# Own and early values in one 64-row product: a memory-augmented recurrent attention kernel

## Chip, cores and metric

The kernel runs on one core of a Trainium2 chip. The metric is the device time of one execution in microseconds; the median of several runs is given.

## The reference

`h = x + A(layernorm(x))`, `out = h + B(layernorm(h))`, with x of 2048 tokens by 640, bf16.

B is a gated feed-forward: `(relu(n @ W_gate) * (n @ W_up)) @ W_down`, with 1728 hidden columns.

A is attention over segments of 32 tokens, one after the other, 32 heads of 128. Each segment sees 8 memory rows, and its first 8 output rows are the memory of the next:

```python
mem = mem0
for s in range(n_seg):                      # 64 segments of 32
    h = concatenate([mem, x[:, 32*s:32*s+32]], axis=1)      # 8 + 32 rows
    q, k, v = h @ Wq, h @ Wk, h @ Wv                        # 32 heads of 128
    scores = where(idx_q < 8 or idx_q >= idx_k, q @ k.T * scale, -1e9)
    o = (softmax(scores) @ v) @ Wo
    mem = o[:, :8]
    outs.append(o[:, 8:])
```

So memory rows see all 40 keys, and a token sees the memory and the tokens up to itself. The chain from `mem` to the next `mem` is serial over 64 segments.

## The kernel before

The weights Wq, Wk, Wv and Wo stay in SBUF. A segment's 40 keys are split in two sets. The *own* keys are the 8 memory rows and the first 24 tokens, 32 rows that need the new memory. The *early* keys are the last 8 tokens (RID = 24) of four consecutive segments, 32 rows that need no memory; their K, Q and V (`Ke`, `Qe`, `Ve`) are computed once for four segments, in units (`extra_units`, `filler`) that lie between the steps of the segments before. In every fourth segment the gaps are filled with `woe_pass`, the output product of early rows.

All these products use tiles of 128 rows by 32 columns: four column groups run side by side, and the four groups g of eight heads each come out in the partitions 32g to 32g + 31. A head is written (k, g), k from 0 to 7.

A segment s of the main loop (line 898) goes, in the order of the code:

- K product (`project`, L374) in two halves, each copied from PSUM by ScalarE (`to_tok`, L395, into `tok[0]`, `tok[1]`) and transposed by VectorE into `Ko` (`flip`, L390).
- `pv_x(s - 1, 0)` (L629 to L643): values for the 32 token rows of the segment before. For each head one product with the own values (`Vp`) and one with the early values (`Ve`), 32 rows each, on tiles of 32x32; the second is added to the first in PSUM. Row group g writes bank b0 + g. 64 matmuls.
- `norm_x` (L645): reciprocal and two multiplications on VectorE into `ox`; `flip_ox` (L532) later transposes `ox` into `oT`.
- Q product, its copies into `tok[2]`, `tok[3]` and flips; half of the V product, copied to `Vp` by ScalarE (`to_v`).
- `scores` (L450) half 0, the second half of V, `scores` half 1: 32 products of 128x32 by 40 columns a half, own keys (a = 0) at column offset 0 and early keys (a = 1) at 160.
- `exp_mem`, `mask_mem`, `pv_mem` (L505), `norm_mem`, `flip_mem`: the 8 memory queries, both halves; between them `exp_x`, `mask_x` for the 32 token queries, and fillers on TensorE.
- `wo_split` (L560), `fold_split`, `wo_pass` (L547), `to_act_split` (L593): the output product, which gives the next segment's memory rows in `act_r`; `rows_split` and `store_attn` send the token rows to DRAM.

The program order is written out by hand. `_Graph` derives the semaphores: each operation waits for the writers and readers of its keys on other engines and for DMAs; every engine runs its own operations in order. SP issues nearly all DMAs, in the order of the code. `store_attn` issues four per segment, and every fourth segment adds a DMA transpose of the next normalised rows and a load.

The first segment is handled in a prologue (L859 to L896) while the last weights are loaded. After segment 63 the feed-forward follows, whose weights are loaded in pieces (`load_piece`) during segments 62 and 63.

Of the kernel before, what the change touches and what calls it, by code (L numbers as in the profile page):

```python
# [163 lines left out]
def build_kernel(nc, A_x, A_mem0, A_Wq, A_Wk, A_Wv, A_Wo, A_seg_len, B_W_gate, B_W_up, B_W_down, out):  # L164
# [57 lines left out]
    mca = ar.alloc("mca", [128, 5, SEG], BF16)  # L222
    act_r = [ar.alloc(f"act_r{i}", [128, 4, DC, 32], BF16) for i in range(2)]
    act_e = [ar.alloc(f"act_e{i}", [128, DC, 32], BF16) for i in range(2)]
    tok = [ar.alloc(f"tok{i}", [128, 512], BF16) for i in range(4)]
# [5 lines left out]
    Vp = [ar.alloc(f"Vp{i}", [128, 8, VW], BF16) for i in range(2)]  # L231
# [8 lines left out]
    ox = ar.alloc("ox", [128, 4, 2, Dh], BF16)  # L240
    wtok = [ar.alloc(f"wtok{i}", [128, DC, 32], BF16) for i in range(2)]
# [36 lines left out]
    for i in (1, 0):  # L278
        add("pool", lambda p, i=i: p.memset(wtok[i][:], 0.0), w=[("wtok", i)])
# [4 lines left out]
    for i in range(2):  # L284
        add("dve", lambda v, i=i: v.memset(oT[i][:], 0.0), w=[("oT", i, n, kh) for n in "mx" for kh in range(2)])
        add("pool", lambda p, i=i: p.memset(act_r[i][:], 0.0),
            w=[("act", i, j, "m") for j in range(4)] + [("act", i, "x")] + [("act", i, "x", j) for j in range(4)])
        add("pool", lambda p, i=i: p.memset(ap(Vp[i], Dh, [[VW, 8], [1, VW - Dh]]), 1.0), w=[("Vp1", i)])
        add("pool", lambda p, i=i: p.memset(ap(Ve[i], Dh, [[VW, 8], [1, VW - Dh]]), 1.0), w=[("Ve1", i)])
        add("pool", lambda p, i=i: p.memset(act_e[i][:], 0.0), w=[("acte", i)])  # L290

    add("pool", lambda p: p.memset(mca[:], BIG), w=[("mca",)])
    for g in range(4):
        for n in range(5):
            sl = mca[32 * g:32 * g + 32, n, :]
            add("pool", lambda p, sl=sl, n=n: p.affine_select(sl, sl, [[1, SEG]], ALU.is_ge, 0.0,
                                                              base=M if n == 0 else M * (n - 1) - RID,
                                                              channel_multiplier=-1), r=[("mca",)], w=[("mca",)])
            if n > 1:
                add("pool", lambda p, sl=sl, n=n: p.affine_select(sl, sl, [[0, SEG]], ALU.is_ge, 0.0,  # L300
                                                                  base=-M * (n - 1), channel_multiplier=1),
                    r=[("mca",)], w=[("mca",)])
    add("pool", lambda p: p.memset(mbd[:], 0.0), w=[("mbd",)])
    for g in range(4):
        add("pool", lambda p, g=g: p.memset(mbd[32 * g:32 * g + 32, :, 8 * g:8 * g + 8], BIG), r=[("mbd",)], w=[("mbd",)])
        for n in range(1, 5):
            sl = mbd[32 * g:32 * g + 32, n, :]
            add("pool", lambda p, sl=sl, n=n: p.affine_select(sl, sl, [[0, 32]], ALU.is_ge, 0.0, base=-M * (n - 1),
                                                              channel_multiplier=1), r=[("mbd",)], w=[("mbd",)])
            add("pool", lambda p, sl=sl, n=n: p.affine_select(sl, sl, [[0, 32]], ALU.is_ge, 0.0, base=M * n - 1,  # L310
                                                              channel_multiplier=-1), r=[("mbd",)], w=[("mbd",)])
# [51 lines left out]
    def project(act, akeys, j, halves, banks, chunks=range(5)):  # L363

        def f(pe):
            for c in chunks:
                for n, i in enumerate(halves):
                    for g in range(4):
                        o = 2048 * i
                        w = (W[:, j, c, o + 512 * g:o + 512 * g + 512] if j == 2 else  # L370
                             W[:, j, c, o:o + 2048].rearrange("p (h e) -> p h e", e=128)[:, :, 32 * g:32 * g + 32])
                        a = (bank(banks[n])[32 * g:32 * g + 32, :], act[:, c, :], w)
                        if n == 0 or not HOLD:
                            ins = pe.matmul(*a, start=(c == 0), stop=(c == DC - 1), skip_group_check=True)  # L374
                        else:
                            ins = again(pe, *a, c == 0, c == DC - 1, g)
            return ins
        add("pe", f, r=list(akeys) + [("W", j, c) for c in chunks], w=[B(b) for b in banks] + [("Wdone", j)])
# [71 lines left out]
    def scores(s, hf):  # L450

        p, _ = place(s)

        def f(pe):
            for k in range(4 * hf, 4 * hf + 4):
                for a in range(2):
                    for g in range(4):
                        h = head(k, g)
                        o = 160 * a + 40 * (k % 4)
                        i = pe.matmul(bank((P0, P1)[hf])[32 * g:32 * g + 32, o:o + 40],  # L460
                                      (Ko if a == 0 else Ke[p])[:, h, :], Qo[:, h, :], start=True, stop=True,
                                      skip_group_check=True)
            return i
        add("pe", f, r=[("Ko", hf), ("Qo", hf), ("Qo", "e"), ("Ke", p, hf)], w=[B((P0, P1)[hf])])
# [9 lines left out]
    def exp_mem(s, hf):  # L474
        _, j = place(s)
        add("act", lambda a: a.activation(ap(Pm, 32 * hf, [[64, 2], [8, 4], [1, 8]]), s_view(hf, 0, M), ACTF.Exp,
                                          scale=SCALE), r=[B((P0, P1)[hf])], w=[("Pm", hf)])

    def mask_mem(s, hf):
        _, j = place(s)  # L480
        for i in (1, 0):
            add("dve", lambda v, i=i: v.tensor_tensor(ap(Pbd, 256 * i + 128 * hf, [[32, 4], [8, 4], [1, 8]]),
                                                      ap(Pm, 64 * i + 32 * hf, [[8, 4], [0, 4], [1, 8]]),
                                                      ap(mbd, 32 * (1 + j) * i, [[0, 4], [8, 4], [1, 8]]), ALU.min),
# [7 lines left out]
    def mask_x(s):  # L492
# [3 lines left out]
                                             ap(mca, 0, [[32 * (1 + j), 2], [0, 8], [1, 32]]), ALU.min),  # L496
            r=[("Px", 0), ("Px", 1), ("mca",)], w=[("Px", 0), ("Px", 1)])

    def v_of(s, a):
        par, p = s % 2, place(s)[0]  # L500
        if a == 0:
            return Vp[par], [("Vp", par, i) for i in range(2)] + [("Vp1", par)]
        return Ve[p], [("Ve", p, i) for i in range(2)] + [("Ve1", p)]

    def pv_mem(s, hf):  # L505
# [10 lines left out]
        (vp, e), par = place(s), s % 2  # L516
        add("pe", f, r=[("Pbd", a, hf) for a in range(2)] + [("Ve", vp, hf), ("Ve1", vp), ("Vp", par, hf), ("Vp1", par)],
# [14 lines left out]
    def flip_ox(s, halves=(0, 1)):  # L532
        p = (s + 1) % 2
        for kh in halves:
            add("dve", lambda v, kh=kh: v.transpose(ap(oT[p], 160 * kh + M, [[320, 4], [40, 4], [1, 32]]),  # L535
                                                       ap(ox, 128 * kh, [[256, 4], [1, 4], [4, 32]])),
                r=[("ox", kh)], w=[("oT", p, "x", kh)])
# [90 lines left out]

    def pv_x(s, b0):  # L629
        (t0, k0), (t1, k1) = v_of(s, 0), v_of(s, 1)  # L630

        def f(pe):
            for kh in range(2):
                for a in range(2):
                    for c in range(4):
                        k = 4 * kh + c
                        for g in range(4):
                            i = pe.matmul(bank(b0 + g)[32 * c:32 * c + 32, 129 * kh:129 * kh + 129],  # L638
                                          Px[32 * g:32 * g + 32, 256 * a + 32 * k:256 * a + 32 * k + 32],
                                          (t0, t1)[a][32 * g:32 * g + 32, k, 0:129], start=(a == 0), stop=(a == 1),  # L640
                                          skip_group_check=True, tile_position=(32 * g, 32 * c))
            return i
        add("pe", f, r=[("Px", 0), ("Px", 1)] + k0 + k1, w=[B(b0 + g) for g in range(4)])  # L643

    def norm_x(b0):  # L645
        src = ps[:, b0 * 512:b0 * 512 + 2048].rearrange("p (g r) -> p g r", r=512)[:, :, 0:258].rearrange(
            "p g (k d) -> p g k d", d=129)
        add("dve", lambda v: v.reciprocal(rx[:, :].rearrange("p (g k) -> p g k", k=2), src[:, :, :, 128]),
            r=[B(b0 + g) for g in range(4)], w=[("rx",)])
        for kh in range(2):  # L650
            add("dve", lambda v, kh=kh: v.tensor_tensor(ox[:, :, kh, :], src[:, :, kh, 0:128],  # L651
                                                      ap(rx, kh, [[2, 4], [0, 128]]), ALU.mult),
                r=[B(b0 + g) for g in range(4)] + [("rx",)], w=[("ox", kh)])
# [35 lines left out]
    for g in range(4):  # L689
        dma(wtok[1][32 * g:32 * g + M, :, :],  # L690
            mem0_ap.rearrange("t (c g j) -> g t c j", g=4, j=32)[g], r=[("wtok", 1)], w=[("wtok0", g)], eng="act")
# [18 lines left out]
    copy_op("dve", w0, wtok[1][:].rearrange("p c t -> p (c t)"), [("wtok", 1)] + [("wtok0", g) for g in range(4)],  # L710
# [156 lines left out]
    for n in range(2):  # L867
        for i in range(2):
            to_v(OB[2][n][i], Vp[0] if n else Ve[1], i, ("Vp", 0) if n else ("Ve", 1), ("act", "dve")[i])
# [3 lines left out]
    pv_x(0, P0)  # L873
# [4 lines left out]
    norm_x(P0)  # L878
    flip_ox(0)
# [18 lines left out]
    for s in range(1, NSEG):  # L898
# [16 lines left out]
        if s > 0:  # L915
            a, ks = pass_act(s)
            for i in range(2):
                project(a, ks, 1, (i,), ((P2, P3)[i],))
                to_tok((P2, P3)[i], i, "act")
                if last and i == 1:  # L920
                    load_piece(("tok", i), "act")
# [10 lines left out]
            if s > 1:  # L932
                pv_x(s - 1, 0)
                norm_x(0)
# [5 lines left out]
            if s > 1:  # L940
                flip_ox(s - 1, (0,))
# [4 lines left out]
            to_v(P2, Vp[par], 0, ("Vp", par), "act")  # L946
            if last:
                load_piece(("Vp", par, 0), "act")
# [10 lines left out]
        if last:  # L959
            to_v(P3, Vp[par], 1, ("Vp", par), "act")  # L960
# [12 lines left out]
        if s > 0:  # L973
            if s > 1:
                flip_ox(s - 1, (1,))
            to_v(P3, Vp[par], 1, ("Vp", par), "act")
# [41 lines left out]
        if s >= 1:  # L1018
            rows_split(P3, P1, wtok[par], ("wtok", par))
            store_attn(wtok[par], ("wtok", par), M, 32 * (s - 1), RID)  # L1020
# [222 lines left out]
```

## Time and profile before

| | |
|---|---|
| median of 3 runs | 1027.08 us (1026.67 to 1027.17) |
| the profiled execution | 1026.84 us |
| its span, first to last instruction | 1025.1 us |
| mean granted TensorE clock | 0.998 |
| one segment, in three of four | 12.4 us |

In the profile a row's first number after the bar or the start is a duration; PE is TensorE, PEld its weight loads, DVE VectorE, ACT ScalarE, POOL GpSimd, SP the queue that issues DMAs (SPq). Names such as L638 are lines of the kernel, given with the function above. In the chain of waits and in the timeline, rows start with the time since the first instruction and the duration, both in us; "x64" is a number of instructions merged into one row. The ends of matmuls are modelled, so TensorE's pace is read from starts.

### The profile page before, as it was taken

The page shows a single profiled execution, that of the slowest core. Times are in us where ns is not written, and L with a number is a line of the kernel's source. Part 1 is how long each engine was busy: PE and PEld are TensorE (multiplying, and loading weights), DVE is VectorE, ACT ScalarE, POOL GpSimd, SP SyncE. Part 2 cuts the span into 40 slices and gives each one's busy share as a digit, 9 for nine tenths or more (in the row PEclk, how much of TensorE's full clock was granted, in tenths as well). Part 3 has the DMA queues.
Part 4 walks back from the last instruction along what each step waited for, and adds up shares of the span by engine and source line. Part 5 has one row for each costly group of instructions (what it writes and reads, how often), then busy time and mean ns, then how long its engine had stood idle before and what let it go on. Part 6 is the DMA issues. An engine that isn't in the chain of part 4 may idle for free.

```text
span 1025.1 us, 57915 instructions
## 1 busy us (share of the span) xinstructions
PE 994.6 (97%) x27201; PEld 559.5 (55%) x26104; DVE 716.0 (70%) x1796; ACT 501.5 (49%) x1262; POOL 168.8 (16%) x402
## 2 busy tenths in 40 slices
PE   4789999999999999999999999999999999999998
PEld 1255656565656565656565566656565554444443
DVE  2558787878778787888888778787777765355332
ACT  1345555555555555565556555555555542121220
POOL 6020202120202020222222222121210010000000
PEclk9999999999999999999999999999999999999999
DMA  9920100010001001111212111000000048413100
GB/s 372 416 68 6 21 7 21 7 22 7 21 7 22 7 21 12 29 18 23 46 27 32 28 32 22 20 8 16 9 6 8 8 114 242 130 27 90 27 14 26
DMA packets 58531, 52.23 MB, mean 51 GB/s; under 512 B 37840, under 2 KB 55216, under 8 KB 56368
## 3 DMA queue, kind: packets, MB, share of 16 engines
q1 hardware_dynamic: 56160, 47.23, 16.7%
q8 instruction: 208, 3.41, 1.4%
q10 hardware_dynamic: 2128, 1.31, 0.5%
q14 instruction: 35, 0.29, 0.1%
HBM read 37.04 MB, written 6.55 MB: 43 GB/s over the span
## 4 chain that ended last, share of the span: by engine, by line
PE 93%; SPq 3%; DMA 2%; issue 0%; DVE 0%; ACT 0%; DVEq 0%; ACTq 0%
PE ps L374 47%; PE ps L817 11%; PE ps L555 7%; PE ps L572 7%; PE ps L357 6%; PE ps L638 4%; PE ps L615 4%; SPq L320 3%; PE ps L1049 3%; PE ps L460 3%; DMA Wo<-in_A_Wo_dram 2%; PE ps L513 2%; PE ps L830 0%; PE ps L1061 0%; DVE TBf L595 0%
## 5 line engine op out<-in xcount | busy, mean ns | idle before, releaser
L374 PE MATMUL ps<-W,act_r 128*32 128x512 bf16 x7580 | 448.3, 381 | 2.1 <-DVE act_r L596 1.4
L374 PEld LDWEIGHTS ps<-W,act_r 128*32 128x32 bf16 x7580 | 190.6, 96 | 201.5 <-DVE act_r L596 31.2
L395 ACT ACTIVATE tok<-ps 128x512 bf16<-128x512 f32 x324 | 189.0, 597 | 163.5 <-PE ps L374 134.4
L374 PE MATMUL ps<-W,act_e 128*32 128x512 bf16 x1224 | 121.2, 383 | 7.5 <-DMA W<-in_A_Wv_dram 4.0
L468 POOL COPY Qo<-Qe 128x256 bf16<-128x256 bf16 x64 | 31.8, 497 | 547.4 <-DVE oT L529 524.4
L390 DVE STREAM_TRANSPOSE Ko<-tok 128x512 bf16<-128x512 bf16 x128 | 89.6, 701 | 40.0 <-ACT tok L395 36.9
L395 ACT ACTIVATE Vp<-ps 128x512 bf16<-128x512 f32 x127 | 75.8, 597 | 69.2 <-PE ps L374 69.2
L390 DVE STREAM_TRANSPOSE Qo<-tok 128x512 bf16<-128x512 bf16 x126 | 88.9, 706 | 14.1 <-ACT tok L395 14.1
L535 DVE STREAM_TRANSPOSE oT<-ox 128x512 bf16<-128x512 bf16 x128 | 87.8, 687 | 0.0
L357 PE MATMUL ps<-W,act_e 128*32 128x512 bf16 x856 | 87.7, 385 | 0.0
L555 PE MATMUL ps<-Wo,oT 128*32 128x160 bf16 x4032 | 83.3, 233 | 1.0 <-issue 0.6
L651 DVE TENSOR_TENSOR ox<-ps,rx 128x512 bf16<-128x512 f32 x128 | 82.5, 687 | 2.2
L572 PE MATMUL ps<-Wo,oT 128*32 128x320 bf16 x2016 | 81.2, 299 | 0.0
L555 PEld LDWEIGHTS ps<-Wo,oT 128*32 128x32 bf16 x4032 | 75.7, 97 | 5.8 <-DMA Wo<-in_A_Wo_dram 1.3
L585 ACT ACTIVATE SA<-TA 64x40 f32<-64x40 f32 x126 | 29.5, 234 | 84.9 <-DVE TA L583 84.2
L845 ACT ACTIVATE g<-ps 128x512 bf16<-128x512 f32 x52 | 30.1, 593 | 82.8 <-PE ps L817 82.8
L817 PE MATMUL ps<-xn2T,Wu 128*128 128x512 bf16 x260 | 64.6, 379 | 0.0
L846 DVE TENSOR_TENSOR hT<-g,ps 128x512 bf16<-128x512 bf16 x52 | 35.8, 688 | 40.5 <-PE ps L817 40.1
L572 PEld LDWEIGHTS ps<-Wo,oT 128*32 128x32 bf16 x2016 | 56.4, 96 | 13.8 <-issue 1.1
L374 PEld LDWEIGHTS ps<-W,act_e 128*32 128x32 bf16 x1224 | 37.1, 97 | 47.8 <-issue 34.8
L817 PE MATMUL ps<-xn2T,Wg 128*128 128x512 bf16 x246 | 61.6, 379 | 1.5 <-issue 1.1
L529 DVE STREAM_TRANSPOSE oT<-om 128x128 bf16<-128x128 bf16 x126 | 39.2, 311 | 29.4 <-ACT om L524 28.1
(109 smaller groups left out, 1359.1 us busy)
## 6 DMA issues: line engine op xcount, KB each, us to landing
W<-in_A_Wk_dram SPq DMA_DIRECT2D x5, 1024.0 KB
W<-in_A_Wq_dram SPq DMA_DIRECT2D x5, 1024.0 KB
W<-in_A_Wv_dram SPq DMA_DIRECT2D x5, 1024.0 KB
Wo<-in_A_Wo_dram SPq DMA_DIRECT2D x8, 640.0 KB
attn_d<-wtok SPq DMA_DIRECT2D x248, 7.5 KB
xt<-in_A_x_dram SPq DMA_DIRECT2D x16, 160.0 KB
at<-attn_d SPq DMA_DIRECT2D x16, 160.0 KB
out_dram<-osb SPq DMA_DIRECT2D x15, 160.0 KB
```

What stands on the lines that cost most here:

```text
L357: return pe.add_instruction(mybir.InstMatmult(name=nc.get_next_instruction_name(), engine=mybir.EngineType.PE, ins=[pe.lower_ap(rhs), pe.l ...
L374: ins = pe.matmul(*a, start=(c == 0), stop=(c == DC - 1), skip_group_check=True)
L390: add("dve", lambda v: v.transpose(dst[:, 16 * i:16 * i + 16, 0:32], tok[t][:, :].rearrange("p (h f) -> p h f", f=32)), r=[("tok", t)], w= ...
L395: add("act", lambda a: a.activation(dst, src, ACTF.Copy), r=r, w=w)
L529: add("dve", lambda v: v.transpose(ap(oT[par], 160 * hf, [[40, 4], [320, 4], [1, 8]]), ap(om, 128 * hf, [[1, 4], [4, 32]])), r=[("om", hf) ...
L535: add("dve", lambda v, kh=kh: v.transpose(ap(oT[p], 160 * kh + M, [[320, 4], [40, 4], [1, 32]]), ap(ox, 128 * kh, [[256, 4], [1, 4], [4, 3 ...
L555: i = pe.matmul(bank(bk)[32 * gg:32 * gg + 32, 0:160], src[:, hb, 0:32], w[:, gg], start=(hb == CH[16 * halves[0]]), stop=(hb == CH[-1]), ...
L572: i = pe.matmul(bank(bk)[32 * q:32 * q + 32, 0:320], src[:, hb, 0:32], w, start=(n == 0), stop=(n == 7), skip_group_check=True)
L615: ins = pe.matmul(bank(bk)[32 * q:32 * q + 32, 0:320], src[:, hb, 0:32], w[:, 2 * (q % 2):2 * (q % 2) + 2], start=(i == 0), stop=(i == 15) ...
L638: i = pe.matmul(bank(b0 + g)[32 * c:32 * c + 32, 129 * kh:129 * kh + 129], Px[32 * g:32 * g + 32, 256 * a + 32 * k:256 * a + 32 * k + 32], ...
L651: add("dve", lambda v, kh=kh: v.tensor_tensor(ox[:, :, kh, :], src[:, :, kh, 0:128], ap(rx, kh, [[2, 4], [0, 128]]), ALU.mult), r=[B(b0 + ...
L817: ins = pe.matmul(bank(bk), w[:, c, lo:lo + 128], xn2T[par][:, c, :], start=(c == 0), stop=(c == DC - 1))
```

## The change

In `scores` the early keys of group g are written to the partitions of the neighbouring group g ^ 1, and the column offset is now chosen by the parity of g. So in the slot of parity r, the partitions 64u to 64u + 63 hold own and early scores of the same head (group 2u + r), in one order for r = 0 and in the other for r = 1. The early values come out swapped in the same way (`project` with `swap`), and the masks `mca` and `mbd` are laid out to match. Two tiles `VM[0]` and `VM[1]` hold own and early values of a head in 64 partitions; `merge_v` fills them by DMA, four copies of 32 partitions x 2080 bytes from `Vp` in each segment and four from `Ve` in every fourth. `pv_x` then makes one product of 64 rows per head: 32 matmuls on tiles of 64x32, with no adding in PSUM.

To make room, `Vp` and `wtok` become single buffers, and `ox` (now `tox`) shares memory with `tok[0]` and `tok[1]`. The second half of `norm_x` moves behind the first half of the Q flips. `pv_x(0)` moves from the prologue into segment 1.

The core of the diff (allocations, memsets and key names of the same kind left out):

```diff
-    mca = ar.alloc("mca", [128, 5, SEG], BF16)
+    mca = ar.alloc("mca", [128, 4, 2, SEG], BF16)
+    tox = ar.alloc("tox", [128, 4, 2, Dh], BF16)
+    tok = [tox[:].rearrange("p g k d -> p (g k d)")[:, 512 * i:512 * i + 512] for i in range(2)]
+    tok += [ar.alloc(f"tok{i}", [128, 512], BF16)[:, :] for i in range(2, 4)]
-    Vp = [ar.alloc(f"Vp{i}", [128, 8, VW], BF16) for i in range(2)]
+    Vp = ar.alloc("Vp", [128, 8, VW], BF16)
+    VM = [ar.alloc(f"VM{i}", [128, 8, VW], BF16) for i in range(2)]
...
     def project(act, akeys, j, halves, banks, chunks=range(5)):
+        swap = 1 if j == 2 and akeys[0][0] == "acte" else 0
...
-                        w = (W[:, j, c, o + 512 * g:o + 512 * g + 512] if j == 2 else
+                        w = (W[:, j, c, o + 512 * (g ^ swap):o + 512 * (g ^ swap) + 512] if j == 2 else
...
                         h = head(k, g)
-                        o = 160 * a + 40 * (k % 4)
-                        i = pe.matmul(bank((P0, P1)[hf])[32 * g:32 * g + 32, o:o + 40],
+                        o, q = 160 * (g % 2) + 40 * (k % 4), 32 * (g ^ a)
+                        i = pe.matmul(bank((P0, P1)[hf])[q:q + 32, o:o + 40],
...
+    def merge_v(s, a):
+        (t, ks), flat = v_of(s, a), "p k d -> p (k d)"
+        for r in range(2):
+            for g in range(4):
+                if g % 2 == r ^ a:
+                    dma(VM[r][32 * g:32 * g + 32].rearrange(flat), t[32 * g:32 * g + 32].rearrange(flat), r=ks,
+                        w=[("VM", r, g)])
+
     def pv_x(s, b0):
...
-                for a in range(2):
+                for r in range(2):
                     for c in range(4):
                         k = 4 * kh + c
-                        for g in range(4):
-                            i = pe.matmul(bank(b0 + g)[32 * c:32 * c + 32, 129 * kh:129 * kh + 129],
-                                          Px[32 * g:32 * g + 32, 256 * a + 32 * k:256 * a + 32 * k + 32],
-                                          (t0, t1)[a][32 * g:32 * g + 32, k, 0:129], start=(a == 0), stop=(a == 1),
-                                          skip_group_check=True, tile_position=(32 * g, 32 * c))
+                        for u in range(2):
+                            i = pe.matmul(bank(b0 + 2 * u + r)[32 * c:32 * c + 32, 129 * kh:129 * kh + 129],
+                                          Px[64 * u:64 * u + 64, 256 * r + 32 * k:256 * r + 32 * k + 32],
+                                          VM[r][64 * u:64 * u + 64, k, 0:129], start=True, stop=True,
+                                          skip_group_check=True, tile_position=(64 * u, 32 * c))
...
     mask_x(0)
     pv_mem(0, 0)
     pv_mem(0, 1)
-    pv_x(0, P0)
+    for a in (1, 0):
+        merge_v(0, a)
...
-    norm_x(P0)
-    flip_ox(0)
...
-            if s > 1:
-                pv_x(s - 1, 0)
-                norm_x(0)
+            pv_x(s - 1, 0)
+            norm_x(0, (0,))
+            if s % 4 == 2:
+                merge_v(s, 1)
             if not last:
                 for i in range(2):
                     project(a, ks, 0, (i,), ((P0, P1)[i],))
                     to_tok((P0, P1)[i], 2 + i, "act")
                     flip(2 + i, Qo, i, [("Qo", i)])
+                    if i == 0:
+                        norm_x(0, (1,))
...
-            if s > 1:
-                flip_ox(s - 1, (1,))
-            to_v(P3, Vp[par], 1, ("Vp", par), "act")
+            flip_ox(s - 1, (1,))
+            to_v(P3, Vp, 1, ("Vp",), "act")
+            merge_v(s, 0)
```

## The prediction

> **What bounds the kernel.** I read the page first, then the chain of waits through four segments, then one segment's timeline. The page:
>
> ```profile
> PE 994.6 (97%) x27201; PEld 559.5 (55%) x26104; DVE 716.0 (70%) x1796; ACT 501.5 (49%) x1262; POOL 168.8 (16%) x402
> PE 93%; SPq 3%; DMA 2%; issue 0%; DVE 0%; ACT 0%; DVEq 0%; ACTq 0%
> PE ps L374 47%; PE ps L817 11%; PE ps L555 7%; PE ps L572 7%; PE ps L357 6%; PE ps L638 4%; PE ps L615 4%; SPq L320 3%; PE ps L1049 3%; PE ps L460 3%; DMA Wo<-in_A_Wo_dram 2%; PE ps L513 2%; PE ps L830 0%; PE ps L1061 0%; DVE TBf L595 0%
> ```
>
> The end is set by TensorE. L638 (`pv_x`) is 4% of the chain, about 41 us; L460 (`scores`) 3%. In the chain of waits (start, duration, what):
>
> ```profile
> 405.34 2.20 PE ps L374 x40
> 407.54 0.66 PE ps L638 x64
> 408.20 3.35 PE ps L374 x60
> 411.56 0.25 PE ps L460 x32
> ```
>
> No wait stands between pieces: a segment lasts 12.4 us (L638 starts at 395.07 and 407.47; one segment of four takes 0.1 to 0.6 more) because its products take that long. A shorter `pv_x` shortens the segment if nothing else becomes late. The timeline at `pv_x`:
>
> ```profile
> 407.47 0.28 PE L638 MATMUL ps<-Vp,Px 32*32 32x129 bf16 x16
> 407.54 0.28 PE L638 MATMUL ps<-Ve,Px 32*32 32x129 bf16 x16
> 407.72 0.35 PE L638 MATMUL ps<-Vp,Px 32*32 32x129 bf16 x16
> 407.86 0.35 PE L638 MATMUL ps<-Ve,Px 32*32 32x129 bf16 x16
> 408.13 0.61 PE L374 MATMUL ps<-W,act_r 128*32 128x512 bf16 x8
> ```
>
> The first column is what matters. Two rounds of 16 matmuls start 0.07 us apart; then comes a pause (0.18 us between starts); then 32 matmuls start evenly, 0.14 us for 16, or 8.5 ns each; the next product starts 0.27 us after the last round's first, of which 0.13 is its own 16 starts and 0.14 the change back to 128-row tiles. So the 0.66 us is not streaming (129 columns need 129/512 of the 0.215 us between rounds of L374, 0.054): it is the count of instructions, a pause and the change of tiles.
>
> **The product.** It has 32 matmuls instead of 64: four rounds of eight, each on eight tiles of 64x32. That two row halves run side by side is seen in `down_tails`, four 64-row matmuls on two halves:
>
> ```profile
> 880.18 0.45 PE L1061 MATMUL ps<-Wd,hT 64*128 64x320 bf16 x4
> 880.56 0.31 PE L1049 MATMUL ps<-Wd,hT 128*128 128x320 bf16 x1
> ```
>
> 0.38 us from start to start; L1049 and L357 start 0.136 apart at the same 320 columns, so two rounds are 0.27, the change 0.1, and four in turn would be 0.54. New length: three round spacings of 0.07, eight starts at about 4 ns (0.03), the change (0.14): **0.38 us**, 0.28 less. Bounds: 0.34 if rounds follow at 0.054; 0.49 if the pause (0.18 - 0.07 = 0.11) comes once; 0.71 if at all three round changes. I take 0.38, because the first 32 matmuls of before ran without pause and there are now 32. Saved: 63 products (`pv_x(1)` to `pv_x(63)`) x 0.28 = **17.6 us**.
>
> The Trainium skill ("TensorE: Matmul & The Clock Gate", Architectural detail) gives TensorE a queue of 64 instructions; by that rule the 32 matmuls and 32 weight loads fit whole and the pause falls away. The trace agrees so far: it comes behind just 32 pairs.
>
> **Scores.** Same 32 matmuls per call, other order: a round of four starts each 0.025 us, and a column group now comes back after two others instead of three, at times. Starts within a round are about 3.4 ns apart, so two rounds lose at most 7 ns, a call 0.027, a segment 0.054. Nothing, if the supply of instructions limits the call's end; I take half, 62 x 0.027 = **+1.7 us**.
>
> **VectorE.** This is the cover that nearly goes. Order now (before):
>
> ```profile
> 408.22 0.71 DVE L390 STREAM_TRANSPOSE Ko<-tok 128x512 bf16<-128x512 bf16 x1 [0.37 <-ACT tok L395]
> 409.06 1.29 DVE L651 TENSOR_TENSOR ox<-ps,rx 128x512 bf16<-128x512 f32 x2
> 410.26 0.70 DVE L390 STREAM_TRANSPOSE Qo<-tok 128x512 bf16<-128x512 bf16 x1
> 411.16 0.71 DVE L390 STREAM_TRANSPOSE Qo<-tok 128x512 bf16<-128x512 bf16 x1 [0.19 <-ACT tok L395]
> 411.79 0.67 DVE L535 STREAM_TRANSPOSE oT<-ox 128x512 bf16<-128x512 bf16 x1
> 412.39 0.33 DVE L482 TENSOR_TENSOR Pbd<-Pm,mbd 128x128 bf16<-128x128 bf16 x2
> 412.96 0.12 PEld L513 LDWEIGHTS ps<-Ve,Pbd 128*32 128x32 bf16 x4
> ```
>
> The K flip hangs on work ahead of `pv_x` and does not move. The second half of `norm_x` goes behind the first Q flip. New times: norm 0 at 409.06 to 409.75; Q0's copy ends at 409.77 (0.28 earlier), flip to 410.5; norm 1 to 411.1; second Q flip to 411.8; `flip_ox` to 412.4; `mask_mem` to 412.63. TensorE wants `pv_mem` at 412.96 - 0.28 = 412.68: 0.05 to spare. So VectorE lets about 0.3 us through, and a still shorter product would win little. Behind it the second `flip_ox` holds the reciprocal of `norm_mem` at 413.25 (413.33 before), and `flip_mem` ends at 414.2 where TensorE's `wo_split` wants 414.17; in the segments with the next units of early keys `flip_mem` has 0.4 to spare (426.86 against 427.28). I take 0.02 a segment, **+1.2 us**; bounds 0 and 0.05 (3.1). That half of the norm frees banks 0 to 3 some 0.8 us later, at 411.1; `pv_mem` writes there at 412.7. `mask_mem`, `exp_mem` and `mask_x` keep their element counts: nothing, they hide behind TensorE.
>
> **Copies.** Four DMAs of 32 x 2080 bytes a segment, four more in each fourth, all on SP's queue. SP issues one in 0.29 to 0.38 us (four stores in 1.51). The trace's semaphore records put a 7.5 KB store's landing 1.3 us after issue. The copy waits for the second half of V (`to_v` at 412.94 to 413.54, 0.28 earlier after): issues to 414.8, landing about 416.5; read by `pv_x` at 419.8. SP's rows of the same segment:
>
> ```profile
> 407.40 1.23 SPq L343 DMA_TRANSPOSE at<-xl  x1
> 411.64 0.36 SPq L320 DMA_DIRECT2D xl<-in_A_x_dram  x1
> 418.36 1.51 SPq L320 DMA_DIRECT2D attn_d<-wtok  x4
> ```
>
> The transpose holds SP for 4.2 us (the load waits for it), yet ends before the copy's turn, and the stores behind come 3.5 us later. The fourth segment's other four copies wait for `pv_x` (408.2), with nothing urgent queued behind; the FFN weight pieces of segment 62 are issued 1.5 us later (824.69), first read by the gate product at about 836. TensorE's new waits stand behind a full queue of L374, ScalarE's `to_v` waits for a copy landed eight us earlier. `wtok` as a single buffer is stored a segment before it is written. All nothing; if a landing took 5 us from the last issue, the cover would be gone.
>
> **Start.** `pv_x(0)` leaves the prologue, which waits for the last Wo load anyway (it lands at 55.53): no gain. Segment 1 takes it: 0.38 plus little, **+0.4 us**; up to 1 us more if its eight copies, queued behind Wo, miss 59.4. POOL's 12 more selects, 0.27 us apart, and 4 more memsets push the end of its setup from 23.7 to about 28, first wanted at 33.8: nothing.
>
> **Sum.** -17.6 + 1.7 + 1.2 + 0.4 = -14.3 us. The profiled execution took 1026.84 (span 1025.1 and 1.7 around it), 0.24 below the median of 1027.08; so 1012.5 for a profiled one and **1012.8** as the median.
>
> **Rivals.**
> - *The pause stays* (0.24): it lies where the first 64 results end and other columns of the banks begin, so it may belong to that place and not to the queue. Product 0.49, 63 x 0.17 = 10.7 saved, scores at their full 3.3: 1020. For it: it is the same in nearly every segment. Against: `down_tails` changes banks without one.
> - *The array was full already* (0.07): 64 matmuls on 16 tiles and 32 on 8 are four rounds both ways, so the streaming time is unchanged; with drains at each round the product stays at 0.66 and the extras of 2.1 us remain: 1029. Against: 0.28 us of rounds is not what fills 0.66. "TensorEngine Tiling (Array Packing)", Theoretical Speedup, of the Trainium skill speaks for it: both small dimensions up to 16 times, one of 64 only twice; by it the change brings nothing.
> - *The copies come late, slower* (0.11): `pv_x`, between the K and Q products, waits for VM. It decides from 5 us between the last issue (414.8) and landing (419.8). At 6 us it costs 1 us in 62 segments, less 0.23: +48, 1075. For it: the transpose took 4.2 us, copies from SBUF to SBUF of this form are not in the trace. Against: the stores' 1.3 us, and DMA engines nearly idle (34 GB/s in this segment).
>
> **Numbers.** Forecast 0.58, rivals 0.24, 0.07, 0.11. A difference under 0.2% can't be told from none here. Faster is the forecast and the pause, 0.82; the full array is 0.06 same and 0.01 slower; slower with the copies 0.12. Range: low, the shortest product (0.34) cut to VectorE's 0.3: 62 x 0.3 = 18.6, 1008; high, the pause with VectorE's 3.1 and the late first copies: 1024. The last two rivals, 0.18, lie outside.
>
> **What would show it.** Four groups of `pv_x` starts 0.07 apart and 0.38 us in the chain; segments of 12.17 us; `mask_mem` ending 0.05 before `pv_mem`; no wait of TensorE for a DMA of VM past segment 1; L460 near 0.26 a call. A gap between the groups says the pause; "PEld ... <- DMA VM" says the copies; TensorE idle on Pbd or oT says VectorE.

## The result, and the profile after

The changed kernel took **1012.12 us** (median of 6 runs, 1010.18 to 1017.05) beside 1027.14 for the kernel before (6 runs, 1026.67 to 1027.45): a ratio of **0.9861, 95% interval 0.9839 to 0.9884**. Forecast were 1012.8 us, and 1008 to 1024. The profiled execution took 1012.74 us with a span of 1011.0, 14.1 less than before's 1025.1. The page of the changed kernel, its first line of engines and its chain that ended last, by engine and by line:

```profile
PE 974.5 (96%) x25153; PEld 540.7 (53%) x24056; DVE 709.8 (70%) x1796; ACT 501.6 (50%) x1262; POOL 171.4 (17%) x416
PE 92%; SPq 3%; DMA 3%; issue 1%; DVE 1%; ACT 0%; DVEq 0%; ACTq 0%
PE ps L380 47%; PE ps L832 10%; PE ps L561 7%; PE ps L578 7%; PE ps L362 6%; PE ps L621 4%; SPq L325 3%; PE ps L1068 3%; PE ps L466 3%; PE ps L651 2%; DMA Wo<-in_A_Wo_dram 2%; PE ps L519 2%; DMA Wd<-in_B_W_down_dram 0%; PE ps L845 0%; PE ps L1080 0%
```

TensorE sets the end as before. `pv_x`, now L651, has fallen from 4% of the chain to 2%. DMA, issue and VectorE have a point more each. (Lines have moved: K, Q and V products L380, `scores` L466, `pv_mem` L519, `mask_mem` L488, `norm_x` L666, `flip_ox` L541.) The chain of waits through one segment, as start, duration, what:

```profile
398.67 2.20 PE ps L380 x40
400.87 0.35 PE ps L651 x32
401.22 3.35 PE ps L380 x60
404.57 0.25 PE ps L466 x32
```

The pieces around `pv_x` have their old lengths, 2.20, 3.35 and 0.25; only the 0.66 has become 0.35. The segment takes 12.09 us instead of 12.40. The same segment's timeline, TensorE and VectorE:

```profile
400.80 0.42 PE L651 MATMUL ps<-VM,Px 64*32 64x129 bf16 x32
...
402.39 0.69 DVE L666 TENSOR_TENSOR tox<-ps,rx 128x512 bf16<-128x512 f32 x1
...
403.73 0.65 DVE L666 TENSOR_TENSOR tox<-ps,rx 128x512 bf16<-128x512 f32 x1
...
404.92 0.67 DVE L541 STREAM_TRANSPOSE oT<-tox 128x512 bf16<-128x512 bf16 x1
405.51 0.32 DVE L488 TENSOR_TENSOR Pbd<-Pm,mbd 128x128 bf16<-128x128 bf16 x2
...
405.98 0.12 PEld L519 LDWEIGHTS ps<-Ve,Pbd 128*32 128x32 bf16 x4
```

The four groups of before are a single row of 32: in the single records (medians over the products) they start 0.067, 0.057 and 0.056 us apart with no pause, all 32 within 0.204 us, and the next product starts 0.147 us after the last of them. On VectorE the second multiplication of `norm_x` stands between the Q flips, as the prediction had it; `mask_mem` ends at 405.83, 0.15 us before `pv_mem` loads its first weights.

Three products of 63 waited. The chain of waits at the first of them:

```profile
495.72 2.23 PE ps L380 x40
...
499.25 0.42 PE ps L651 x32
```

L380 ends at 497.95, and `pv_x` starts 1.30 us later. The chain puts ScalarE's work between them, which `pv_x` doesn't read; what it lacked was VM. The trace records the landing of each copy in sixteen reports. The last report of the fourth copy came at 499.15, and the product's first weight load started 0.06 us later; it is 0.06 us at the other two as well. Counted from start to start, against the usual 0.31 us behind the last matmul of L380 (L832 at the last `pv_x`), the waits are 1.40 us here, 1.32 at 597.99 and 0.63 at 829.26, the last `pv_x`; 3.3 us in all. SP's timeline ahead of the first:

```profile
489.72 0.34 SPq L325 DMA_DIRECT2D at<-attn_d  x1
490.11 1.63 SPq L325 DMA_DIRECT2D attn_d<-wtok  x4
493.53 0.34 SPq L325 DMA_DIRECT2D h_d<-xt  x1
493.97 2.46 SPq L325 DMA_DIRECT2D VM<-Vp  x4
```

The store of `h_d` stands ahead of the copies in SP's order. It waits for POOL's addition, which runs from 492.10 to 493.50, and that waits for the load of `at`, issued only at 489.72. So SP stood still from 491.74 to 493.53, with the four copies behind the store. They also take long to issue, 0.62 us each (2.46 for four); over the whole trace 30 of 324 copies took more than 1 us, up to 1.9.

The late issue alone would have cost hardly 0.1 us. Half of the loop's copies landed in full within 2.04 us of their issue; by that the last one, issued at 495.85, would have been there at 497.89, about when TensorE wanted it. Fifteen of its reports had come by 497.82, the sixteenth came 1.33 us later. Such late landings are common: 70 of 316 copies took more than 3 us. At 597.99 it was the same: last issue at 594.64, fifteen reports by 597.26, the last at 597.89. At 829.26 no store of `h_d` stands ahead; the last copy, issued at 824.25, took 4.92 us. What delays the last report is not known.

### The profile page after: what moved, and what is told of

It is laid out like the page before. It is cut to its first block, busy times and chain, and to the rows that moved or that the text cites. A ratio compares the mean times of both kernels' runs of the same rounds, so it can differ in the third digit from the quotient of the medians.

```text
span 1011.0 us, 54369 instructions
## 1 busy us (share of the span) xinstructions
PE 974.5 (96%) x25153; PEld 540.7 (53%) x24056; DVE 709.8 (70%) x1796; ACT 501.6 (50%) x1262; POOL 171.4 (17%) x416
## 4 chain that ended last, share of the span: by engine, by line
PE 92%; SPq 3%; DMA 3%; issue 1%; DVE 1%; ACT 0%; DVEq 0%; ACTq 0%
PE ps L380 47%; PE ps L832 10%; PE ps L561 7%; PE ps L578 7%; PE ps L362 6%; PE ps L621 4%; SPq L325 3%; PE ps L1068 3%; PE ps L466 3%; PE ps L651 2%; DMA Wo<-in_A_Wo_dram 2%; PE ps L519 2%; DMA Wd<-in_B_W_down_dram 0%; PE ps L845 0%; PE ps L1080 0%
## 5 line engine op out<-in xcount | busy, mean ns | idle before, releaser
L380 PE MATMUL ps<-W,act_r 128*32 128x512 bf16 x7580 | 448.1, 380 | 1.6 <-DVE act_r L602 1.1
L380 PEld LDWEIGHTS ps<-W,act_r 128*32 128x32 bf16 x7580 | 192.8, 96 | 200.8 <-DVE act_r L602 30.8
L401 ACT ACTIVATE tok<-ps 128x512 bf16<-128x512 f32 x190 | 109.9, 597 | 92.0 <-PE ps L380 83.1
L380 PE MATMUL ps<-W,act_e 128*32 128x512 bf16 x1224 | 121.2, 384 | 8.7 <-DMA W<-in_A_Wv_dram 5.1
L396 DVE STREAM_TRANSPOSE Ko<-tox 128x512 bf16<-128x512 bf16 x128 | 89.6, 702 | 39.7 <-ACT tox L401 38.8
L401 ACT ACTIVATE tox<-ps 128x512 bf16<-128x512 f32 x134 | 79.6, 598 | 53.2 <-PE ps L380 33.3
L541 DVE STREAM_TRANSPOSE oT<-tox 128x512 bf16<-128x512 bf16 x128 | 87.8, 687 | 0.1
L666 DVE TENSOR_TENSOR tox<-ps,rx 128x512 bf16<-128x512 f32 x128 | 86.1, 672 | 2.3
L832 PE MATMUL ps<-xn2T,Wu 128*128 128x512 bf16 x259 | 64.5, 379 | 0.1
L832 PE MATMUL ps<-xn2T,Wg 128*128 128x512 bf16 x247 | 61.8, 379 | 1.3 <-issue 1.0
L380 PEld LDWEIGHTS ps<-W,act_e 128*32 128x32 bf16 x1224 | 36.9, 97 | 48.4 <-issue 31.2
```

The costliest lines, as they stand in the source:

```text
L396: add("dve", lambda v: v.transpose(dst[:, 16 * i:16 * i + 16, 0:32], tok[t][:, :].rearrange("p (h f) -> p h f", f=32)), r=[("tok", t)], w= ...
L401: add("act", lambda a: a.activation(dst, src, ACTF.Copy), r=r, w=w)
L666: add("dve", lambda v, kh=kh: v.tensor_tensor(tox[:, :, kh, :], src[:, :, kh, 0:128], ap(rx, kh, [[2, 4], [0, 128]]), ALU.mult), r=[B(b0 + ...
L832: ins = pe.matmul(bank(bk), w[:, c, lo:lo + 128], xn2T[par][:, c, :], start=(c == 0), stop=(c == DC - 1))
```

## The experiments

Two sets ran, each with its own runs of the kernel before: e2, e3, e4 and e6 beside 1026.90 us, the others beside 1026.53. Line numbers and diffs are against the changed kernel. From each kernel's one profile, a single execution, three stretches were read off: the time to the first `scores` of segment 1 (start), from there to those of segment 62 (loop), and the rest.

| kernel | us | start | loop | rest | plain segment |
|---|---|---|---|---|---|
| before | 1027.14 | 62.6 | 761.1 | 201.4 | 12.40 |
| changed | 1012.12 | 64.2 | 744.1 | 202.7 | 12.09 |
| changed, second set | 1013.59 | 64.1 | 745.6 | 204.2 | 12.09 |
| e1, no copies in the loop | 1008.19 | 63.9 | 740.5 | 202.0 | 12.09 |
| e2, old product, no copies | 1026.94 | 62.9 | 759.6 | 202.1 | 12.40 |
| e3, old product, all copies | 1034.82 | 64.7 | 767.1 | 202.5 | 12.40 |
| e4, new product run twice | 1034.57 | 65.4 | 766.1 | 201.8 | 12.40 |
| e5, norm in one piece | 1015.04 | 64.2 | 747.8 | 200.4 | 12.14 |
| e6, no product, no copies | 996.00 | 64.5 | 727.1 | 203.0 | 11.88 |
| e7, store behind the copies | 1011.27 | 63.7 | 741.5 | 201.4 | 12.09 |

**e2, the change without its product.** No `merge_v` anywhere, and the product of 64 matmuls from `Vp` and `Ve`; merged tiles' scores, split norm and everything else stay.

```diff
-                for r in range(2):
+                for a in range(2):
+                    t = v_of(s, a)[0]
                     for c in range(4):
                         k = 4 * kh + c
-                        for u in range(2):
...
+                        for g in range(4):
+                            o = 256 * ((g + a) % 2) + 32 * k
+                            i = pe.matmul(bank(b0 + g)[32 * c:32 * c + 32, 129 * kh:129 * kh + 129],
+                                          Px[32 * g:32 * g + 32, o:o + 32],
+                                          t[32 * g:32 * g + 32, k, 0:129], start=(a == 0), stop=(a == 1),
```

> The changed kernel with its product put back to 64 matmuls on tiles of 32x32 (read straight from Vp and Ve, the early half added to the neighbouring group's bank, so heads are mixed) and with all copies left out. Everything else of the change stays: the order of scores, of norm_x, the single buffers. Theory (the gain is the product's alone): 0.66 us per product again, segments of 12.40 us, time within 2 us of the kernel before, 1025 to 1029. Rival (part of the gain comes from the moved norm_x or the other order of scores): 5 us or more below the kernel before.

Measured: 1026.94 us (1026.14 to 1027.86), ratio 1.0001 (0.9992 to 1.0011); the plain segment is back at 12.40. Reordered scores, moved norm, extra selects and shared buffers neither cost nor bring anything that can be told in the time; in this one profile the loop is 1.5 us shorter than before's, and start and rest together are 1.0 longer. e1 below has the new product and, like e2, no copies in the loop: its loop is 19.1 us shorter than e2's, 61 segments of 0.31 us. The gain is the product's alone.

**e3, the old product and the copies as well.** As e2, but every `merge_v` stays, and `pv_x` waits for VM without reading it.

```diff
-        add("pe", f, r=[("Px", 0), ("Px", 1)] + [("VM", r, g) for r in range(2) for g in range(4)],
+        add("pe", f, r=[("Px", 0), ("Px", 1)] + v_of(s, 0)[1] + v_of(s, 1)[1] + [("VM", r, g) for r in range(2) for g in range(4)],
```

> As e2_old_product, but with the copies issued as in the changed kernel, and the product waiting for them though it doesn't read them. Theory (the copies cost what the changed kernel's trace shows: Wo lands 1.5 us later, two or three late landings of 1.3 us, less here since segments are longer): 2 to 5 us above e2_old_product. Rival (the copies are hidden but for the start): 1.5 us above or less.

Measured: 1034.82 us (1034.20 to 1036.36), ratio 1.0079 (1.0064 to 1.0094): 7.9 us more than e2, where 2 to 5 were expected. In the profile the start is 1.8 us longer, the loop 7.5. Late copies make up 2.4 us of the loop (waits of 1.5, 0.6 and 0.3 us). Another 3 us lie in seven gaps inside a function's matmuls, such as the one ahead of this row of TensorE's timeline:

```profile
321.87 0.31 PE L621 MATMUL ps<-Wo,oTe 128*32 128x320 bf16 x1 [0.55 <-issue]
```

"issue" says that the profile shows nothing that the engine waited for. The copies aren't shown to be the cause: the loop of the kernel before, without copies, has three such gaps (0.2 us or more) with 1.2 us, and the changed kernel, with copies, has one of 0.3 us in its first profile and none in its second. Some 2 us of the 7.5 aren't accounted for.

**e4, the new product run twice.** Each matmul is issued a second time with the same result, so 64 matmuls on 64-row tiles.

```diff
-            for kh in range(2):
+            for kh in (0, 1, 0, 1):
```

> The changed kernel with every product of pv_x issued twice in a row (same results): 64 matmuls of 64 rows. Theory (the pause belongs to the supply of instructions and comes after 32 pairs, with 8.3 ns a pair behind it): length 0.35 + 0.11 + 32 x 0.0083 = about 0.70 to 0.73 us, 63 x 0.36 = 23 us above the changed kernel, about 1035. Rival (the pause belonged to adding in PSUM or to 32-row tiles, rounds go on at 0.053): 0.35 + 4 x 0.053 = 0.56 us, 13 us above it, about 1025, and no gap after the 32nd matmul.

Measured: 1034.57 us (1033.25 to 1035.78), ratio 1.0075 (1.0060 to 1.0090). Its chain of waits:

```profile
397.03 2.34 PE ps L380 x40
399.37 0.67 PE ps L651 x64
400.04 3.35 PE ps L380 x57
```

64 matmuls of 64 rows take what 64 of 32 rows took: 0.67 against 0.66 us (0.70 to 0.73 were expected), and the segment is back at 12.40. In single records the first 32 start within 0.204 us, the 33rd starts 0.254 us after the first (before: 0.252), and the rest follow 8.3 ns apart in both. The change of columns at the 17th and at the 49th brings no pause, so it isn't the place in the banks that makes it. The second 32 add 0.32 us to the product, what the change saves (0.31).

**e6, no product at all.** `pv_x` of segments 1 to 62 and the loop's copies are left out, so the token values of these segments aren't computed.

```diff
-            pv_x(s - 1, 0)
+            if s == 1:
+                pv_x(s - 1, 0)
```

> The changed kernel with the products of segments 1 to 62 left out (62 x 0.35 = 21.7 us of TensorE) and the copies of all segments but the first left out too; VectorE still does norm_x and flip_ox on what lies in the banks. Theory (VectorE caps the gain soon: mask_mem ends 0.15 us before pv_mem in the changed kernel's trace): segments shrink by 0.15 from 12.10 and TensorE waits on Pbd, about 1000. Rival (no cap, VectorE's work moves along): segments of 11.75, about 987.

Measured: 996.00 us (994.96 to 996.91), ratio 0.9699 (0.9684 to 0.9713). The plain segment gives back 0.21 us of the product's 0.35, where 0.15 was expected: 11.88. Its chain of waits:

```profile
396.67 0.69 DVE tox L666
397.36 0.62 DVE Qo L396
397.98 0.58 DVE tox L666
398.55 0.61 DVE Qo L396
399.17 0.59 DVE oT L541
399.76 0.25 DVE Pbd L488 x2
400.01 0.04 issue
400.06 0.30 PE ps L519 x8
```

From the K flip to `pv_mem` the chain is VectorE without a gap, in the very order that the prediction wrote down. This is the limit that it named; it lies 0.21 us below the present segment.

**The changed kernel again**, so that the second set has its own.

> The changed kernel itself, to stand beside the next three on the same chip. 1010 to 1017 as before, with runs that differ by several us.

Measured: 1013.59 us (1012.57 to 1015.93), ratio 0.9876 (0.9859 to 0.9893). Its table of waits names the late copies:

```profile
PE ps L651 <- DMA VM<-Vp: 2.4, 2, 1.6
```

That is 2.4 us in two products, 1.6 at most. By the starts four products waited, 3.5 us in all, each until the last report of a copy: 1.7 us at 499.80 and 0.9 at 598.83 behind a store of `h_d`, 0.3 at 279.17 and 0.5 at 611.55 without one. At these two one of the copies had taken 1.5 or 1.6 us to issue, and the last one 3.8 and 4.0 us to land.

**e1, the new product without the loop's copies.** The three `merge_v` calls in the loop are gone, those of the prologue stay, so the values are of the first segment throughout.

```diff
-            if s % 4 == 2:
-                merge_v(s, 1)
...
-            merge_v(s, 0)
...
-            merge_v(s, 0)
```

> The changed kernel with the copies left out in all segments but the first, so the product reads old values. Theory (the copies are what spreads the runs and what lies between the 19 us that shorter segments give and the 15 us measured): 1007 to 1009, runs within 1 us of each other, no wait of TensorE ahead of the product; the start stays 1.5 us late. Rival (the spread and the loss come from elsewhere): 1012 with the same spread.

Measured: 1008.19 us (1008.16 to 1009.67), ratio 0.9824 (0.9809 to 0.9838), 5.4 us below the changed kernel beside it. No product waits, and the loop is 20.6 us shorter than before's. The spread of its runs is 1.5 us (1 was expected) where the changed kernel's was 6.9 and 3.4.

**e5, the norm in one piece.** Both multiplications directly behind `pv_x`, as before the change.

```diff
-            norm_x(0, (0,))
+            norm_x(0)
...
-                    if i == 0:
-                        norm_x(0, (1,))
-            else:
-                norm_x(0, (1,))
```

> The changed kernel with both halves of norm_x ahead of the Q flips, as in the kernel before. Theory (the moved half only just matters): the first Q flip ends at 404.31 on the clock of the changed trace where scores want it at 404.36, so no change, within 2 us. Rival (the moved half is what lets the shorter product through): scores wait 0.1 us or more in each segment, 6 us or more above the changed kernel.

Measured: 1015.04 us (1014.27 to 1016.06), ratio 0.9887 (0.9873 to 0.9902): 1.45 us more than the changed kernel, in overlapping intervals, so the times alone don't tell them apart. The profile does: the table of waits has a row that the changed kernel lacks,

```profile
PEld ps L466 <- DVE Qo L396: 23.2, 58, 0.4
```

a wait of the scores' weight loads for the second Q flip in 58 segments. Loads run ahead, so most of the 0.4 us is hidden: the first `scores` take 0.29 instead of 0.25, the segment 12.14. So the time stayed within the 2 us expected, but the moved half isn't free: 0.05 us a segment are some 3 us over the loop.

**e7, the copies' way made free.** The store of `h_d` moves behind the copies, and one FFN weight piece of the last segment, whose issue waits for `Vp`, moves from ScalarE's queue, ahead of the last copies, to SP's behind them.

```diff
-                dma(h_d[128 * e2:128 * e2 + 128, :], xt[:, :], r=[("xt",)], w=[("h_d", e2)])
...
-            if last:
-                load_piece(("Vp", 0), "act")
...
             merge_v(s, 0)
+            load_piece(("Vp", 0))
...
             merge_v(s, 0)
+            if s % 4 == 0 and e2 is not None:
+                dma(h_d[128 * e2:128 * e2 + 128, :], xt[:, :], r=[("xt",)], w=[("h_d", e2)])
```

> The changed kernel with two DMAs behind the copies on SP's queue instead of ahead: the store of early rows (h_d, four segments) and one FFN weight piece of the last segment (moved from ScalarE's queue). Theory (late copies are a matter of what stands ahead of them): the waits of 1.4, 1.3 and 0.6 us ahead of the product are gone, 2 to 4 us below the changed kernel. Rival (they are late for other reasons, such as slow landings): same as the changed kernel.

Measured: 1011.27 us (1008.67 to 1012.66), ratio 0.9855 (0.9838 to 0.9871), 2.3 us below the changed kernel beside it; the intervals overlap. No `pv_x` waits in its profile, whose span of 1006.7 us is near e1's 1006.5. But the profiled execution was the fastest of its four, 2.6 us ahead of the next; whether products waited in the others isn't known. Late landings are as frequent in this profile as in the changed kernel's (64 of 316 copies over 3 us) and find room, the tightest with 0.08 us. It beats the kernel before clearly, the changed kernel only by its medians.

## Why the prediction was right

The total was right and so was the mechanism of the gain; several sizes were off, in opposite directions, and nearly cancel. Forecast was a profiled execution 14.3 us shorter; it was 14.1 shorter: loop -17.0, start +1.6, rest +1.3. Of the rest, the last wait makes 0.6; the stretch differs by 3.8 us between kernels whose code there is nearly the same, so the remainder can't be told from scatter.

- **The product: undersized by 2 us.** Forecast 0.38 us, measured 0.35. The mis-sized term is the spacing of the groups: 0.07 was taken from the pairs of before, 0.060 came on average. 0.35 lies near the lower bound (0.34). 63 x 0.31 = 19.5 instead of 17.6.
- **The pause.** It went, as forecast. It hung on the count of instructions: e4 puts 64 on the new tiles and the 33rd again starts 0.25 us behind the first. So the rival that tied it to the place in the banks falls. What "TensorE: Matmul & The Clock Gate" (Architectural detail) of the Trainium skill says of a queue of 64 instructions fits: 32 pairs go through at once. That the queue is the reason, no run shows.
- **The full array** fell. Four rounds of tiles both ways, yet 0.66 against 0.35; and with 64 matmuls eight rounds on eight tiles take what four rounds on sixteen took. The equal speed that the prediction worked out by "TensorEngine Tiling (Array Packing)" (Theoretical Speedup) of the Trainium skill didn't come: 0.35 us against 0.66.
- **Scores: forecast +1.7, cost nothing.** `scores` keeps 0.25 us a call in the chain. Of the two cases that the prediction left open, this fits the one in which the supply of instructions sets the call's end; no run tests it.
- **VectorE: forecast +1.2, cost nothing.** `mask_mem` has 0.15 us to spare where 0.05 was worked out: VectorE's five steps ran 0.13 us faster than laid out. That limit is real but later: e6 meets it 0.21 us below the present segment. With the 0.31 already gained, VectorE lets 0.52 us through, not 0.3.
- **Copies: forecast nothing, cost 3.3 us.** Both prices came from small stores and were too low: issue took 0.62 us each, not 0.29 to 0.38, and landing 2.04 us in the median, over 3 us in more than a fifth of the copies, instead of 1.3. The stores read for the price had this tail too: in before's trace three of the four issued from 418.36 on have their last report 2.9 to 3.3 us after issue. In the segment of the prediction VM is there at 411.05 and wanted at 412.99, 1.9 us to spare instead of 3.3; the median over the segments is 1.6. The step that failed was to take one segment's order on SP and one store's landing for all: in two of the four segments with an `h_d` store SP waits for POOL ahead of the copies, and with a late landing on top the spare time is gone. Before's table of waits had SP's wait:

```profile
SPq L320 <- POOL xt L662: 11.7, 4, 3.1
```

The third rival, slow landing, thus came true in part: its landing of 5 us was nearly reached once (4.92), and 3 products of 63 waited instead of 62. e1's loop is 3.6 and 5.1 us shorter than in the two profiles of the changed kernel, and e1 took 5.4 us less as a median. In e7's profile the waits are gone with the order; that the weight piece caused the last one was not tried alone.
- **Start: forecast +0.4, cost 1.6.** The prediction named late first copies for up to 1 us, but not this way. The chain of waits at the start has, first in the changed kernel, then in e2:

```profile
35.39 21.66 DMA Wo<-in_A_Wo_dram
```

```profile
35.46 20.03 DMA Wo<-in_A_Wo_dram
```

The eight first copies, issued behind the last Wo loads, run beside them: from 54 to 56 us the DMA engines move 223 GB/s where before moved 83, and Wo lands at 57.05 instead of 55.53. All the kernels with these copies have a later start than e2, by 0.8 us or more. POOL's longer setup shows no cost: e2 has it too and starts 0.3 us behind before, with the first product now inside. (It is 14 instructions more, 12 selects and 2 memsets; the 4 new memsets replace 2.)

So the gains were 5 us too small (product 1.9, scores 1.7, VectorE 1.2) and the costs nearly as much too small (start 1.2, late copies 3.3); that they cancel is luck. The range would have held either error alone: e1, with none of the waits, stands at its lower end, 1008.

## What to carry to other kernels

For short bursts of small-tile matmuls count instructions, not columns: read the starts, see where they go from dense to sparse, and ask whether the burst can be cut to what goes through at once. A DMA that replaces engine work costs nothing only if its queue is followed through every kind of segment: look for what stands ahead of it that waits for a slow engine, and take its issue time and its landing from many DMAs of the same shape, the latest of them included. A cap found by laying out a neighbour's order by hand is worth testing by leaving the whole step out.

## What the hardware showed that was not expected

- In `pv_x` the first 32 pairs of weight load and small matmul start within 0.14 us on 32-row tiles and 0.20 us on 64-row tiles; the rest follow 8.3 ns apart from 0.25 us after the first start, on both alike (before and e4).
- A copy of 32 x 2080 bytes from SBUF to SBUF held SP's queue for 0.62 us, where the 7.5 KB stores beside it take 0.38. It landed 2.04 us after issue in the median, and 70 of 316 in more than 3 us; in most of these one of the sixteen landing reports comes long after the others. Why stays open.
- Copies issued later on the same queue put off an earlier load's landing by 1.5 us (Wo at 57.05 against 55.53).
- Gaps without a shown cause lie inside runs of matmuls, with and without the copies: 3 us in e3's loop, 1.2 in before's, 0.3 and none in the changed kernel's. This stays open.
